# Where the sums of the seven accumulators stand: ahead of the next group's first products, and, in the last group, between the accumulators' own closing products

## The chip, the cores and the metric

The kernel runs on one core of one Trainium2 chip. The metric is device time in microseconds (us), as the median of several runs. "The profiled execution" is one run that a hardware profiler recorded; every duration of a single instruction below comes from it. In its rows PE is the engine of the matrix multiplications (TensorE), PEld its loading of weights, DVE is VectorE, ACT is ScalarE, POOL is GpSimd and SP is SyncE, which issues most DMAs here.

## The reference: what is computed

A state space scan over 4 batches, 8 heads, 768 positions and 32 values per head gives a matrix of 3072 tokens by 256 features. A feed-forward block follows it, all in float32:

```
h = x @ w_in                            # 3072x256 @ 256x2048
g = h * (1.0 / (1.0 + np.exp(-1.702 * h)))
out = (g @ w_out).astype(np.float32)    # 3072x2048 @ 2048x256
```

The scan itself works on chunks. With `L` the decay between two positions of a chunk and `state` what is carried on from earlier chunks, its core is

```
CB = np.einsum('bhin,bhjn->bhij', Cc, Bc)
y_intra = np.einsum('bhij,bhjd->bhid', CB * L, xc)
y_inter = np.einsum('bhin,bhnd->bhid', Cc, state) * decay_to_i[:, :, :, None]
state = decay_full[:, :, None, None] * state + np.sum(Bx, axis=2)
```

## The kernel before

The 3072 tokens are cut into six groups of 512 (`g` = 0 to 5). A group of tokens comes out of the scan as two pairs of 128-position chunks (`p`, two per group), whose result is written transposed into `yT`. The scan of a pair is cut into steps: `turn` transposes B and C on PE (tiles `tp`, then `BT`, `CT`, `CsT`), `gain` multiplies B by x on PE (tile `A`, line L438), `keep` turns `A` into the carried state `S` on DVE (L452, L459), `score` multiplies C by B on PE (tile `cb`, L412), `weigh` multiplies `L` by `cb` on DVE (L422), and `finish` makes `y` on PE and copies it to `yT` on ACT.

The feed-forward block of a group has 16 blocks of 128 hidden features. `hidden` (L508) multiplies `yT` by one block of `w_in` into a PSUM tile `h`, and ACT applies the gelu into `gT` (L511); a step H0 to H7 makes two of them. In the groups 1 to 5 the second matrix product is made in Winograd's form of Strassen's scheme: for each pair of blocks `j` (steps P0 to P7) DVE first makes sums of `gT` (`mix_g`, tile `mg`, L557 to L559), sums of `w_out` are made once (`mix_w`, tile `mw`), and `product` (L575) makes seven matrix products of 128 by 128 by 256 instead of eight, one for each of seven accumulators. The program has one matmul for each of them, the profile two records. The accumulators lie in one PSUM tile `acc` of four banks, two to a bank, the seventh alone, and add up over the eight `j`. When the last `j` is done, `combine` puts the seven together: one ACT copy of accumulators 0 and 3 into the tile `u` (L586), then five DVE sums (L592) that read the other accumulators and write the result `c`. `give` transposes `c` on PE (tiles `oT`, L600), scales it on ACT into `ob` (L603) and stores it.

The four banks of `acc` are the only buffer of that size (`area`, one buffer with the tag "cb"): `cb` of the scan's next pair and `acc` take turns in it. So `score` of the next pair can't begin before `combine` has read all of `acc`. The other four banks (`bank`, tag "ff") go round among `h`, `tp`, `A`, `y` and `oT`.

Every engine runs its instructions in the order in which the program was written (`in_order` adds that as a constraint); nothing reorders them. The order around the change is a list of steps for each group, `H0, H1, H2, P0, H3, P1, ... H7, P5, P6, P7`, and a table `after[g]` of further work behind each step. In the groups 2 to 5 the work behind H0 is first `combine` of the group before, then, where there is a next group, `score` and `weigh` of its first pair; behind H1 stand `mix_g(g, 0)`, `give` of the group before, `score` and `weigh` of the second pair. Behind P5 and P6 stand `turn`, `gain` and `keep` of a pair two groups on. After the last group `combine` and `give` follow without anything else.

Of the kernel before, what the change touches and what calls it, by code (L numbers as in the profile page):

```python
# [8 lines left out]
FP32 = mybir.dt.float32  # L9
U32 = mybir.dt.uint32  # L10
AF = mybir.ActivationFunctionType
ALU = mybir.AluOpType
# [3 lines left out]
P = 128  # L16
# [18 lines left out]
def kernel(  # L35
# [28 lines left out]
    nc = tc.nc  # L64
# [4 lines left out]
    NB, NH, S, D = x.shape  # L69
# [3 lines left out]
    T = NB * S  # L73
# [285 lines left out]
    def turn(p):  # L359
        turn_only(p)  # L360
        since_start(p)
# [6 lines left out]
    def area(name):  # L368
        return ps.tile([P, R, 4 * P], FP32, tag="cb", name=name, bufs=1)
# [48 lines left out]
    def weigh(p):  # L418

        L, cb = Ls[p], st[p].pop("cb")  # L420
        Lv = L.rearrange("p k r q i -> p k r (q i)")
        nc.vector.tensor_tensor(out=Lv, in0=Lv, in1=cb.rearrange("p r k e -> p k r e"),  # L422
                                op=ALU.mult)
# [134 lines left out]
        nc.vector.tensor_tensor(out=t[:, 2], in0=B[:, 1, 1], in1=t[:, 0], op=ALU.subtract)  # L558
        nc.vector.tensor_tensor(out=t[:, 3], in0=B[:, 1, 0], in1=t[:, 2], op=ALU.subtract)  # L559

    def product(g, j):
        if j == 0:
            acc[g] = area(f"acc{g}").rearrange("p r (t e) -> p r t e", t=2)
        B = gT.pop((g, j)).rearrange("p i (t e) -> p i t e", t=2)
        T = mixed_g.pop((g, j))
        A, S = w_out[:, 2 * j:2 * j + 2], mixed_w[j]
        for r, t, lhsT, rhs in (
                (0, 0, A[:, 0, :P], B[:, 0, 0]),
                (0, 1, A[:, 1, :P], B[:, 1, 0]),
                (1, 0, S[:, 1], T[:, 2]),  # L570
                (1, 1, S[:, 0], T[:, 0]),
                (2, 0, S[:, 2], T[:, 1]),
                (2, 1, S[:, 3], B[:, 1, 1]),
                (3, 0, A[:, 1, P:], T[:, 3])):
            nc.tensor.matmul(out=acc[g][:, r, t], lhsT=lhsT, rhs=rhs,  # L575
                             start=(j == 0 and t == 0), stop=(j == NF // 2 - 1),
                             skip_group_check=True)

    def combine(g):


        a = acc.pop(g).rearrange("p r t e -> p (r t) e")
        u = ffn.tile([P, 4, HT], FP32, tag="gT", name=f"u{g}", bufs=NF // 2)
        c = done[g] = ffn.tile([P, 2, 2, HT], FP32, tag="gT", name=f"c{g}", bufs=NF // 2)

        nc.scalar.activation(u[:, 0:4:3], a[:, 0:4:3], AF.Copy)  # L586
        for o, v, w in ((u[:, 2], a[:, 2], u[:, 0]),
                        (u[:, 1:3], a[:, 3:5], u[:, 2:3].to_broadcast([P, 2, HT])),
                        (c[:, 0], a[:, 1:6:4], u[:, 0:2]),
                        (c[:, 1, 1], u[:, 2], u[:, 3]),  # L590
                        (c[:, 1, 0], a[:, 6], u[:, 2])):
            nc.vector.tensor_tensor(out=o, in0=v, in1=w, op=ALU.add)  # L592

    def give(g):
        c = done.pop(g)
        for t in range(2):
            o = bank(f"oT{g}_{t}").rearrange("p (k e) -> p k e", k=2)
            for k in range(2):
                for i in range(2):
                    nc.tensor.transpose(out=o[:, k, i * P:(i + 1) * P],  # L600
                                        in_=c[:, i, t, k * P:(k + 1) * P], identity=ident)
            ob = out_tile(g, t)
            nc.scalar.activation(ob, o, AF.Copy, scale=1.0 / GELU_SCALE)  # L603
            store(g, t, ob)
# [45 lines left out]
    def at(places, i, *work):  # L650
        places.setdefault(i, []).extend(work)
# [26 lines left out]
    for g in range(1, NG):  # L678
        n, places = (g + 1) * PG, after[g]
        chunks = range((g + 2) * CG, (g + 3) * CG) if g + 2 < NG else ()  # L680
        if g == 1:
            def late(p):
                gain(p)
                keep(p)
                score(p)
                weigh(p)

            at(places, "H0", lambda: decay(2 * CG), lambda: decay(2 * CG + 1), lambda: turn(n1))
            n1 = n
# [34 lines left out]
    for g in range(1, NG):  # L724
        if g + 2 < NG:
            for k in range(PG):
                load((g + 2) * PG + k)
            for b in range(NB):
                if (g + 2) * CG <= b * NC < (g + 3) * CG:
                    spread_rows(b)  # L730
                    at(after[g], "P4", lambda b=b: clip_rows(b), lambda b=b: decay_rows(b))
        ahead = 5 if g == 1 else 3
        steps = [f"H{j}" for j in range(ahead)]
        for j in range(NF // 2):
            steps += [f"P{j}"] + ([f"H{j + ahead}"] if j + ahead < NF // 2 else [])
# [12 lines left out]
    combine(NG - 1)  # L748
    give(NG - 1)

    in_order(tc)
# [30 lines left out]
```

## Time and profile before

| what | value |
|---|---|
| median of three runs | 430.02 us (429.22 to 431.66) |
| the profiled execution's own time | 429.2 us |
| its span, from the first to the last instruction | 427.5 us |
| PE busy | 395.3 us, 92% of the span |
| DVE busy | 232.5 us, 54% |
| ACT busy | 119.9 us, 28% |
| mean granted clock of PE | 0.947 |

The time that lies around the span is 429.2 - 427.5 = 1.7 us. Busy times are sums over the whole span; a wait in one place doesn't show in them. The granted clock is the share of full speed that PE was given; at 0.50 a matmul takes twice as long.

### The profile page before, as it was taken

How to read it: one execution, taken by the hardware profiler on the slowest of the kernel's cores; microseconds unless marked ns; L12 is line 12 of the kernel's file. 1: busy time of each engine (PE TensorE's matmuls, PEld its weight loads, DVE VectorE, ACT ScalarE, POOL GpSimd, SP SyncE). 2: the span in 40 equal slices, each digit the busy share in tenths (PEclk: the TensorE clock that was granted, in tenths of full speed). 3: DMA queues.
4: the chain of work that ended last, by engine and by line, in shares of the span. 5: the costliest groups of instructions: out<-in, count | busy, mean ns of one | idle time of the engine just before them, and what ended most of it. 6: DMA issues, size and time to landing. Idle time of an engine off the chain costs nothing.

```text
span 427.5 us, 5052 instructions
## 1 busy us (share of the span) xinstructions
PE 395.3 (92%) x2006; PEld 251.5 (59%) x2006; DVE 232.5 (54%) x372; ACT 119.9 (28%) x227; POOL 8.9 (2%) x28
## 2 busy tenths in 40 slices
PE   6789995989999999699999699999699999999993
PEld 2354454868556687266658256668346667566672
DVE  3899889683879694543573462573262221232212
ACT  4129964340422112132122131212122121231211
POOL 4100000000000000000000000000000000000000
PEclk9559996999999999899999899999889999999997
DMA  8889919500897000078000051000010000010001
GB/s 182 169 179 247 328 52 164 179 0 2 131 263 105 20 0 2 0 245 100 2 1 0 2 174 73 0 0 2 0 49 2 2 0 0 0 51 0 0 2 49
DMA packets 86070, 29.65 MB, mean 69 GB/s; under 512 B 75744, under 2 KB 79008, under 8 KB 86048
## 3 DMA queue, kind: packets, MB, share of 16 engines
q1 hardware_dynamic: 83968, 29.07, 28.5%
q10 hardware_dynamic: 2080, 0.26, 0.4%
q8 instruction: 16, 0.26, 0.3%
q14 instruction: 6, 0.05, 0.0%
HBM read 26.08 MB, written 3.24 MB: 69 GB/s over the span
## 4 chain that ended last, share of the span: by engine, by line
PE 84%; DVE 8%; issue 2%; DMA 2%; ACT 2%; SPq 1%; DVEq 0%; POOL 0%; ACTq 0%; POOLq 0%
PE h L508 39%; PE acc L575 29%; PE o L527 5%; PE cb L412 3%; PE y L488 2%; DVE c L592 2%; PE y L480 1%; DMA af<-in_a_dram 1%; DVE u L592 1%; SPq L110 1%; PE oT L600 1%; DVE L L275 1%; PE tp L379 1%; PE ab L292 1%; ACT u L586 1%
## 5 line engine op out<-in xcount | busy, mean ns | idle before, releaser
L508 PE MATMUL h<-yT,w_in 128*128 128x512 f32 x384 | 177.3, 609 | 0.3 <-ACT yT L494 0.3
L508 PEld LDWEIGHTS h<-yT,w_in 128*128 128x128 f32 x384 | 73.6, 195 | 81.8 <-issue 77.2
L511 ACT ACTIVATE gT<-h 128x512 f32<-128x512 f32 x96 | 57.0, 595 | 204.5 <-PE h L508 162.1
L557 DVE TENSOR_TENSOR mg<-gT 128x512 f32<-128x512 f32 x40 | 27.5, 688 | 91.5 <-ACT gT L511 88.4
L575 PE MATMUL acc<-mg,mw 128*128 128x256 f32 x240 | 58.3, 379 | 0.0
L575 PEld LDWEIGHTS acc<-mg,mw 128*128 128x128 f32 x240 | 45.6, 190 | 6.2
L575 PE MATMUL acc<-gT,w_out 128*128 128x256 f32 x160 | 42.1, 386 | 0.0
L275 DVE TENSOR_TENSOR_SCAN L<-a,idents 128x1024 f32<-128x1024 f32 x18 | 41.1, 2283 | 0.0
L575 PEld LDWEIGHTS acc<-gT,w_out 128*128 128x128 f32 x160 | 29.6, 190 | 15.2 <-issue 11.5
L527 PE MATMUL o<-w_out,gT 128*128 128x256 f32 x128 | 32.3, 410 | 0.0
L422 DVE TENSOR_TENSOR L<-L,cb 128x2048 f32<-128x2048 f32 x10 | 22.9, 2285 | 16.1 <-PE cb L412 16.1
L527 PEld LDWEIGHTS o<-w_out,gT 128*128 128x128 f32 x128 | 25.6, 206 | 5.0 <-issue 1.2
L412 PE MATMUL cb<-CT,BT 32*128 32x256 f32 x160 | 17.0, 495 | 11.5 <-DVE c L592 11.5
L592 DVE TENSOR_TENSOR u<-acc,u 128x256 f32<-128x256 f32 (+1 forms) x10 | 5.6, 558 | 36.3 <-ACT u L586 36.1
L575 PE MATMUL acc<-gT,mw 128*128 128x256 f32 x80 | 23.8, 379 | 0.0
L575 PE MATMUL acc<-mg,w_out 128*128 128x256 f32 x80 | 23.8, 379 | 0.0
L412 PEld LDWEIGHTS cb<-CT,BT 32*128 32x128 f32 x160 | 10.9, 231 | 16.3 <-issue 14.7
L559 DVE TENSOR_TENSOR mg<-gT,mg 128x256 f32<-128x256 f32 x40 | 17.0, 425 | 1.4
L558 DVE TENSOR_TENSOR mg<-gT,mg 128x256 f32<-128x256 f32 x40 | 17.0, 424 | 1.4
L575 PEld LDWEIGHTS acc<-gT,mw 128*128 128x128 f32 x80 | 15.2, 190 | 2.1
L575 PEld LDWEIGHTS acc<-mg,w_out 128*128 128x128 f32 x80 | 15.2, 190 | 2.1
L151 ACT ACTIVATE z<-e,edge 128x512 f32<-128x512 uint32 x16 | 11.4, 713 | 12.8 <-DVE e L147 12.8
(87 smaller groups left out, 278.7 us busy)
## 6 DMA issues: line engine op xcount, KB each, us to landing
a<-scratch SPq DMA_DIRECT2D x18, 512.0 KB, 5.5
bits<-in_moe_w_in_dram SPq DMA_DIRECT2D x8, 512.0 KB, 6.0
bits<-in_moe_w_out_dram SPq DMA_DIRECT2D x8, 512.0 KB, 3.8
out_dram<-ob SPq DMA_DIRECT2D x12, 256.0 KB, 2.1
x<-in_x_dram SPq DMA_DIRECT2D x22, 128.0 KB, 3.0
b<-in_B_dram SPq DMA_DIRECT2D x24, 64.0 KB, 5.5
c<-in_C_dram SPq DMA_DIRECT2D x24, 64.0 KB, 3.1
af<-in_a_dram SPq DMA_DIRECT2D x4, 384.0 KB
```

Source lines behind the costliest of these rows:

```text
L151: nc.scalar.activation(z, e, AF.Relu, scale=-8.0, bias=edge[:, 0:1])
L275: nc.vector.tensor_tensor_scan(out=Ls[p][:, k].rearrange("p r q i -> p (r q i)"), data0=ra[n], data1=idents.rearrange("p h i -> p (h i)"), ...
L412: nc.tensor.matmul(out=cb[:, r, k], lhsT=BT[rows, k], rhs=CT[rows, k].rearrange("p q i -> p (q i)"), start=True, stop=True, tile_position= ...
L422: nc.vector.tensor_tensor(out=Lv, in0=Lv, in1=cb.rearrange("p r k e -> p k r e"), op=ALU.mult)
L508: nc.tensor.matmul(out=h, lhsT=w_in[:, k, f * P:(f + 1) * P], rhs=yT[g][:, k], start=(k == 0), stop=(k == NK - 1))
L511: nc.scalar.activation(gT[g, j][:, i], h, AF.Silu, scale=GELU_SCALE)
L527: nc.tensor.matmul(out=o[k // 2][:, k % 2], lhsT=gT[g, f // 2][:, f % 2, k * P:(k + 1) * P], rhs=w_out[:, f], start=(f == 0 and k % 2 == 0 ...
L557: nc.vector.tensor_tensor(out=t[:, 0:2], in0=B[:, :, 1], in1=B[:, 0], op=ALU.subtract)
L558: nc.vector.tensor_tensor(out=t[:, 2], in0=B[:, 1, 1], in1=t[:, 0], op=ALU.subtract)
L559: nc.vector.tensor_tensor(out=t[:, 3], in0=B[:, 1, 0], in1=t[:, 2], op=ALU.subtract)
L575: nc.tensor.matmul(out=acc[g][:, r, t], lhsT=lhsT, rhs=rhs, start=(j == 0 and t == 0), stop=(j == NF // 2 - 1), skip_group_check=True)
L592: nc.vector.tensor_tensor(out=o, in0=v, in1=w, op=ALU.add)
```

## The change

`combine` is called right behind the step list of its group, and no longer behind H0 of the next group. So on ACT its copy stands ahead of the gelu of the next group's first two `h`, and on DVE its five sums stand ahead of what the next group does there. `gain` and `keep` of the second pair, which stood behind P6, move behind H0 of the next group, ahead of `score` of the first pair. The order of two of the five sums is swapped (`c[:, 1, 1]` now precedes `c[:, 0]`), and `give` now takes the second half of the features first.

In the last group the products of P5, P6 and P7 are taken out of the step list. They are made behind it, accumulator by accumulator in the order 0, 3, 2, 4, 1, 5, 6, each for `j` = 5, 6, 7, with those steps of `combine` in between whose accumulators are complete. `give` follows.

```
-    def product(g, j):
+    def product(g, j, only=range(7)):
...
+        for i in only:
+            lhsT, rhs = terms[i]
+            nc.tensor.matmul(out=acc[g][:, i], lhsT=lhsT, rhs=rhs,
+                             start=(j == 0 and i % 2 == 0), stop=(j == NF // 2 - 1),
...
+        sums = ((u[:, 2], a[:, 2], u[:, 0]),
+                (u[:, 1:3], a[:, 3:5], u[:, 2:3].to_broadcast([P, 2, HT])),
+                (c[:, 1, 1], u[:, 2], u[:, 3]),
+                (c[:, 0], a[:, 1:6:4], u[:, 0:2]),
+                (c[:, 1, 0], a[:, 6], u[:, 2]))
+        for i in steps:
+            if i:
+                o, v, w = sums[i - 1]
+                nc.vector.tensor_tensor(out=o, in0=v, in1=w, op=ALU.add)
...
-        for t in range(2):
+        for t in (1, 0):
...
-            at(places, "H0", lambda g=g: combine(g - 1))
             at(places, "H1", lambda g=g: mix_g(g, 0), lambda g=g: give(g - 1))
             if g + 1 < NG:
-                at(places, "H0", lambda n=n: score(n), lambda n=n: weigh(n))
+                at(places, "H0", lambda n=n: gain(n + 1), lambda n=n: keep(n + 1),
+                   lambda n=n: score(n), lambda n=n: weigh(n))
...
-                at(places, f"P{5 + k}", lambda p=p: turn(p), lambda p=p: gain(p),
-                   lambda p=p: keep(p))
+                at(places, f"P{5 + k}", lambda p=p: turn(p))
+                if k == 0:
+                    at(places, "P5", lambda p=p: gain(p), lambda p=p: keep(p))
...
-            else:
+            elif g < NG - 1 or j < 5:
                 product(g, j)
...
-    combine(NG - 1)
+        if g < NG - 1:
+            combine(g)
+
+    for i, n in ((0, ()), (3, (0,)), (2, (1,)), (4, (2, 3)), (1, ()), (5, (4,)), (6, (5,))):
+        for j in range(5, NF // 2):
+            product(NG - 1, j, (i,))
+        if n:
+            combine(NG - 1, n)
     give(NG - 1)
```

The order on ACT where group 1 ends and group 2 begins (`u1` is the copy of group 1's accumulators, `gT2_0` and `gT2_1` are the gelu of group 2's first four `h`). Before:

```order
L511 ACTIVATE gT2_0_1289<-h2_0_1290 128x512
L511 ACTIVATE gT2_0_1289<-h2_1_1294 128x512
L586 ACTIVATE u1_1298<-acc1_1072 128x2x256
L511 ACTIVATE gT2_1_1316<-h2_2_1317 128x512
L511 ACTIVATE gT2_1_1316<-h2_3_1321 128x512
```

Now:

```order
L586 ACTIVATE u1_1255<-acc1_1072 128x2x256
L511 ACTIVATE gT2_0_1283<-h2_0_1284 128x512
L511 ACTIVATE gT2_0_1283<-h2_1_1288 128x512
L511 ACTIVATE gT2_1_1316<-h2_2_1317 128x512
L511 ACTIVATE gT2_1_1316<-h2_3_1321 128x512
```

The copy moved past two gelus. The five sums on DVE, which wait for it, follow right behind it in both programs.

The order on PE in the same place (`A7` is `gain` of the second pair, `cb6` is `score` of the first). Before:

```order
L379 MATMUL tp7_1236<-ident_149,c7_877 128x128 x2
L438 MATMUL A7_1248<-x7_878,Be7_1162 32x64 x8
L575 MATMUL acc1_1072<-gT1_7_1140,w_out_77 128x256 x2
L575 MATMUL acc1_1072<-mg1_7_1232,mw3_1171 128x256 x3
L575 MATMUL acc1_1072<-gT1_7_1140,mw3_1171 128x256
L575 MATMUL acc1_1072<-mg1_7_1232,w_out_77 128x256
L508 MATMUL h2_0_1290<-yT2_985,w_in_76 128x512 x2
L508 MATMUL h2_1_1294<-yT2_985,w_in_76 128x512 x2
L412 MATMUL cb6_1306<-CT6_1207,BT6_1205 128x256 x8
```

Now:

```order
L379 MATMUL tp7_1236<-ident_149,c7_877 128x128 x2
L573 MATMUL acc1_1072<-gT1_7_1140,w_out_77 128x256 x2
L573 MATMUL acc1_1072<-mg1_7_1232,mw3_1171 128x256 x3
L573 MATMUL acc1_1072<-gT1_7_1140,mw3_1171 128x256
L573 MATMUL acc1_1072<-mg1_7_1232,w_out_77 128x256
L508 MATMUL h2_0_1284<-yT2_985,w_in_76 128x512 x2
L508 MATMUL h2_1_1288<-yT2_985,w_in_76 128x512 x2
L438 MATMUL A7_1292<-x7_878,Be7_1162 32x64 x8
L412 MATMUL cb6_1306<-CT6_1207,BT6_1205 128x256 x8
```

Only `A7` changed its place: from before the last products to between the two `h` and `cb6`. The same holds where groups 2 and 3 end.

The closing products of the last group on PE, with the semaphores that each waits for in brackets. Before, the last of the three `j`:

```order
L575 MATMUL acc5_2254<-gT5_7_2346,w_out_77 128x256 [waits Activation_49] x2
L575 MATMUL acc5_2254<-mg5_7_2362,mw3_1171 128x256 [waits DVE_49]
L575 MATMUL acc5_2254<-mg5_7_2362,mw3_1171 128x256 x2
L575 MATMUL acc5_2254<-gT5_7_2346,mw3_1171 128x256
L575 MATMUL acc5_2254<-mg5_7_2362,w_out_77 128x256 [waits DVE_49]
```

Now, from the last product of accumulator 3 on: three each of accumulators 2, 4 and 1, and, behind those of accumulator 5, the first of accumulator 6:

```order
L573 MATMUL acc5_2254<-mg5_7_2355,mw3_1171 128x256 [waits DVE_49]
L573 MATMUL acc5_2254<-mg5_5_2322,mw2_1129 128x256 [waits Activation_49]
L573 MATMUL acc5_2254<-mg5_6_2342,mw3_1171 128x256
L573 MATMUL acc5_2254<-mg5_7_2355,mw3_1171 128x256 [waits DVE_49]
L573 MATMUL acc5_2254<-mg5_5_2322,mw2_1129 128x256 [waits DVE_49]
L573 MATMUL acc5_2254<-mg5_6_2342,mw3_1171 128x256
L573 MATMUL acc5_2254<-mg5_7_2355,mw3_1171 128x256
L573 MATMUL acc5_2254<-gT5_5_2306,w_out_77 128x256 [waits DVE_49]
L573 MATMUL acc5_2254<-gT5_6_2326,w_out_77 128x256
L573 MATMUL acc5_2254<-gT5_7_2346,w_out_77 128x256
...
L573 MATMUL acc5_2254<-mg5_5_2322,w_out_77 128x256 [waits DVE_49]
```

Each accumulator's last product now comes one after the other, and four of the first products wait for ACT or DVE: those of accumulator 2 (for ACT), 4, 1 and 6 (for DVE). Their operands of `j` = 5 had been waited for by earlier rows or come from another engine, so these waits belong to the copy and the sums that read `acc`.

More of the change, by code (lines that the diff above doesn't have):

```diff
@@ L559, in mix_g @@
         nc.vector.tensor_tensor(out=t[:, 3], in0=B[:, 1, 0], in1=t[:, 2], op=ALU.subtract)
-    def product(g, j):
+    def product(g, j, only=range(7)):
         if j == 0:
-            acc[g] = area(f"acc{g}").rearrange("p r (t e) -> p r t e", t=2)
-        B = gT.pop((g, j)).rearrange("p i (t e) -> p i t e", t=2)
-        T = mixed_g.pop((g, j))
+            acc[g] = area(f"acc{g}").rearrange("p r (t e) -> p (r t) e", t=2)
+        B = gT[g, j].rearrange("p i (t e) -> p i t e", t=2)
+        T = mixed_g[g, j]
@@ L566, in product @@
         A, S = w_out[:, 2 * j:2 * j + 2], mixed_w[j]
[L567 to L576, printed above, removed]
-                             skip_group_check=True)
@@ L579, in combine @@
[L579 to L592, printed above, removed]
+        terms = ((A[:, 0, :P], B[:, 0, 0]), (A[:, 1, :P], B[:, 1, 0]), (S[:, 1], T[:, 2]),
+                 (S[:, 0], T[:, 0]), (S[:, 2], T[:, 1]), (S[:, 3], B[:, 1, 1]),
+                 (A[:, 1, P:], T[:, 3]))
@@ new lines, in product, with combine @@
+        for i in only:
+            lhsT, rhs = terms[i]
+            nc.tensor.matmul(out=acc[g][:, i], lhsT=lhsT, rhs=rhs,
+                             start=(j == 0 and i % 2 == 0), stop=(j == NF // 2 - 1),
+                             skip_group_check=True)
+    def combine(g, steps=range(6)):
+        a = acc[g]
+        if 0 in steps:
+            u = ffn.tile([P, 4, HT], FP32, tag="gT", name=f"u{g}", bufs=NF // 2)
+            c = ffn.tile([P, 2, 2, HT], FP32, tag="gT", name=f"c{g}", bufs=NF // 2)
+            done[g] = u, c
+            nc.scalar.activation(u[:, 0:4:3], a[:, 0:4:3], AF.Copy)
+        u, c = done[g]
+        sums = ((u[:, 2], a[:, 2], u[:, 0]),
[7 more added lines that the diff above has]
+                nc.vector.tensor_tensor(out=o, in0=v, in1=w, op=ALU.add)
@@ L594, in give @@
     def give(g):
-        c = done.pop(g)
-        for t in range(2):
+        u, c = done.pop(g)
+        for t in (1, 0):
             o = bank(f"oT{g}_{t}").rearrange("p (k e) -> p k e", k=2)
```

## The prediction

> **What bounds the kernel now.** I read the page's first parts, then the chain of waits, then the list of waits, then the timeline where a group ends. The page says that PE is the bound:
>
> ```profile
> span 427.5 us, 5052 instructions
> PE 395.3 (92%) x2006; PEld 251.5 (59%) x2006; DVE 232.5 (54%) x372; ACT 119.9 (28%) x227; POOL 8.9 (2%) x28
> PE 84%; DVE 8%; issue 2%; DMA 2%; ACT 2%; SPq 1%; DVEq 0%; POOL 0%; ACTq 0%; POOLq 0%
> ```
>
> The last row is the chain: 84% of it is PE's own work, so only the remaining places can give without making products cheaper. The chain around the end of group 1 (start, length, what) and the matching row of the list of waits (total, times, longest):
>
> ```profile
> 168.59 3.45 PE h L508 x8
> 172.08 0.47 issue
> 172.55 0.60 ACT u L586
> 173.18 0.43 DVE u L592
> 173.64 0.70 DVE u L592
> 174.36 1.37 DVE c L592 x3
> 175.86 1.15 PE cb L412 x16
> 177.01 5.33 PE h L508 x8
> ...
> PE cb L412 <- DVE c L592: 11.5, 3, 3.8
> ```
>
> PE finishes its eight records of `h` at 172.04, then stands until 175.86, because `cb` goes into the banks that the sums still read. The sums are late for a reason on ACT: `acc` was complete at about 168.6, but the copy stands behind the gelu of `h1`, which waits for `h`. This happens three times.
>
> The views by stretch show what follows (length; busy PE, PEld, DVE, ACT, POOL; granted clock). The first three rows are the waits, then come in turn `cb` and `h` behind the wait, and the same work for the second pair without a wait:
>
> ```profile
> 172.04:175.86 3.82, 0.00 (x0) 0.03 (x1) 2.47 (x5) 1.08 (x2) 0.00 (x0) 1.00 0.00 0
> 238.07:241.89 3.82, 0.00 (x0) 0.03 (x1) 2.47 (x5) 1.09 (x2) 0.00 (x0) 1.00 0.00 0
> 304.05:307.87 3.82, 0.00 (x0) 0.03 (x1) 2.47 (x5) 1.08 (x2) 0.00 (x0) 0.90 0.00 0
> 175.86:182.17 6.31, 6.31 (x24) 2.91 (x25) 3.74 (x4) 0.60 (x1) 0.00 (x0) 0.73 0.00 0
> 183.14:187.85 4.71, 4.71 (x26) 2.16 (x25) 3.43 (x4) 1.41 (x3) 0.00 (x0) 1.00 0.78 197
> 241.89:248.15 6.26, 6.26 (x24) 3.10 (x25) 3.74 (x4) 0.60 (x1) 0.00 (x0) 0.73 0.01 3
> 249.12:253.83 4.71, 4.71 (x26) 2.16 (x25) 3.43 (x4) 1.40 (x3) 0.00 (x0) 1.00 0.83 195
> 307.87:315.43 7.56, 7.56 (x25) 3.65 (x26) 3.74 (x4) 0.60 (x1) 0.00 (x0) 0.60 0.00 0
> ```
>
> So every wait is paid twice: PE idles 3.82 us, and then the clock falls, and the same work takes 6.31, 6.26 and 7.56 us instead of 4.71.
>
> **Part 1: the sums ahead of the next group, at three boundaries.** When are they done now? The end of the program shows the same copy and sums with nothing ahead of them (start, length):
>
> ```profile
> 418.57 0.59 PE L575 MATMUL acc<-mg,w_out 128*128 128x256 f32 x2
> 419.26 0.60 ACT L586 ACTIVATE u<-acc 128x512 f32<-128x512 f32 x1 [8.53 <-PE acc L575]
> 419.89 1.15 DVE L592 TENSOR_TENSOR u<-acc,u 128x256 f32<-128x256 f32 x2 [7.52 <-ACT u L586]
> 421.07 0.69 DVE L592 TENSOR_TENSOR c<-acc,u 128x512 f32<-128x512 f32 x1
> 422.01 0.42 DVE L592 TENSOR_TENSOR c<-acc,u 128x256 f32<-128x256 f32 x1
> 422.48 1.14 PE L600 MATMUL oT<-ident,c 128*128 128x128 f32 x7 [0.34 <-DVE c L592]
> 423.07 1.19 ACT L603 ACTIVATE ob<-oT 128x512 f32<-128x512 f32 x2 [3.21 <-PE oT L600]
> ```
>
> The copy starts 0.10 us after the last product ends (418.57 + 0.59 = 419.16) and the sums end at 422.43, 3.27 us after it. At the first boundary the last product ends at 168.6, so the sums end at 171.9. PE is busy with `h` until 172.04 and then with `A`, which the change puts there. What that costs stood in the trace at P6:
>
> ```profile
> 164.94 0.43 PE L438 MATMUL A<-x,Be 128*32 128x64 f32 x16
> ```
>
> About 0.4 us, taken from P6 and spent here, so it adds nothing. `cb` can start at about 172.4, with the sums 0.5 us ahead of it. The wait is gone: 3 x 3.82 = **11.46 us**. If the sums were up to 0.5 us later, `A` would still cover them; the cover without `A` is only 0.14 us, about the 0.13 us from the last sum to `cb` before (174.36 + 1.37 to 175.86). From below I take 11.0, from above 11.46.
>
> What is late next? On DVE `keep` now stands between the sums and `weigh`, and waits for `A`; behind it queue `weigh`, then `mix_g`. `keep` took 1.13 us at P6 (its first and its last row), `weigh` takes 2.29:
>
> ```profile
> 166.59 0.48 DVE L452 TENSOR_TENSOR S<-A,own 128x128 f32<-128x128 f32 x2
> 167.37 0.35 DVE L459 SCALAR_TENSOR_TENSOR S<-S,since 128x128 f32<-128x128 f32 x1
> 184.35 2.29 DVE L422 TENSOR_TENSOR L<-L,cb 128x2048 f32<-128x2048 f32 x1 [3.48 <-PE cb L412]
> ```
>
> `A` ends at 172.4, `keep` at 173.9, `cb` at 173.5, so `weigh` starts 0.4 us late and ends at 176.2. Who needs it first is the second `cb`, which PE reaches after `cb` (1.1), `h` (3.6) and `oT` (1.0), at 178.1. The next product needs `mg`, for which the page has 0.69 + 2 x 0.42, so it is done by 177.7; PE came to that product at 189.35, and will at 189.35 - 3.82 - 1.60 = 183.9. Both covers are over 1.5 us; nothing is added. The SP queue only follows: its stores and loads keep their order and hang on `oT`'s copies, which move with PE.
>
> **The clock** is the second term. If PE no longer idles, `cb` and `h` run at 4.71: 1.60 + 1.55 + 2.85 = **6.00 us**. Evidence that a short pause doesn't cost clock, and that unbroken work doesn't either:
>
> ```profile
> 89.85 0.43 PE L438 MATMUL area<-x,Be 128*32 128x64 f32 x16 [1.76 <-DVE CsT L396]
> 88.10:89.90 1.80, 0.05 (x4) 0.05 (x8) 1.66 (x4) 1.46 (x5) 0.00 (x0) 1.00 0.00 0
> 320.00:366.00 46.00, 46.00 (x235) 31.74 (x234) 10.59 (x21) 7.97 (x16) 0.00 (x0) 1.00 0.00 1
> ```
>
> A pause of 1.76 us kept 1.00; the three of 3.82 did not. Bounds: 0 if the dips have another cause, 6.00 as measured; I take 6.00, since each dip begins during or just behind its wait. The Trainium skill says on its page "TensorE: Matmul & The Clock Gate", section "What's actually happening", that an idle window of about 3.4 us halves the clock until about one busy window has passed; this trace agrees, with 3.82 us of idling ahead of each dip. By that figure a dip would cost about half of 3.4 us, 5.1 us for three as an estimate, and the sum below would be 0.9 us smaller.
>
> **Part 2: the boundary between groups 4 and 5** has no scan and no `cb`. There `h` of both H0 and H1 covers the sums almost entirely:
>
> ```profile
> 372.92 0.27 PE L600 MATMUL oT<-ident,c 128*128 128x128 f32 x1
> 373.40 0.98 PE L600 MATMUL oT<-ident,c 128*128 128x128 f32 x7 [0.21 <-DVE c L592]
> 374.22 3.60 PE L508 MATMUL h<-yT,w_in 128*128 128x512 f32 x8
> ```
>
> From `oT` to the next `h` it is 1.30 us here; elsewhere `oT` fills 0.97 (between the stretches above, 182.17 to 183.14, and again 248.15 to 249.12), where nothing waits. Gain **0.33 us** (0 to 0.45).
>
> **Part 3: the end.** One would expect a gain: with the sums between products, only the last sum would follow the last product. In the frame of the old trace, PE could issue the next instruction at 419.0 (two records of 3.02 / 14 = 0.216 us after 418.57; that row stands below), and then come four `oT` (0.5), the other four behind the last sum (0.26 + 0.42 + 0.1 after 419.0, then 0.4), and two copies of 0.6: the last copy ends about 1.9 us after the products, at 420.9 instead of 424.26. That would be 3.4 us.
>
> But four of the products now wait: accumulator 2 for the ACT copy, 4, 1 and 6 for the sum that was issued just before. Each turns PE and ACT or DVE into a chain. A wait lasts from PE's free slot to the reader's start (419.26 - 419.0 = 0.26), plus the reader, plus its way back (422.43 to 422.48 there, 0.13 at `cb`; I take 0.10): copy 0.60 + 0.36 = 0.96; first sum 0.43 + 0.36 = 0.79; second 0.70 + 0.36 = 1.06; the wide one 0.69 + 0.36 = 1.05. Together 3.86. And products behind a pause take 3.22 us per seven, against 3.02 in a row:
>
> ```profile
> 189.35 3.22 PE acc L575 x14
> 197.85 3.02 PE acc L575 x14
> ```
>
> I put 0.1 us on each restart (bounds 0 and 0.2), so 4.26 (3.5 to 4.8). The new end is 419.0 + 4.26 + 1.9 = 425.16 against 424.26: a **loss of 0.9 us** (0.1 to 1.5). Only the one sum that reads no accumulator and part of `oT` are hidden; all else that was serial stays serial, with four extra trips between the engines. Cover and cost change hands again if the waits aren't there: then the 3.4 us gain stands.
>
> **Sum.** 11.46 + 6.00 + 0.33 - 0.9 = 16.9 us. The profiled execution took 429.2, so it would take 412.3. The median of the runs is 430.02, 0.8 above it; applied to that, **413.1 us**.
>
> **The rivals.**
>
> *The tail overlaps after all* (4%). For it: no product needs a sum's result. Against: the rows of the changed order name the waits. Time 413.1 - 4.3 = 408.8.
>
> *The clock falls in the closing products* (12%). There PE would be busy about 1.3 us in every 2.3. The trace has no such stretch late in the program; the pause of 1.76 us kept the clock, which speaks against it, but it stood alone. If the clock halves after the second wait, nine products of 0.43 and the `oT` double: + 4.4, 417.5. The Trainium skill, same page, section "A second HAM failure mode: psum-queue depth-cycling", says that many tiny idle gaps between groups of matmuls can make the clock swing; this is the rule that speaks against the change.
>
> *The wait at `cb` shrinks but stays* (5%): the copy starts only behind the first gelu.
>
> ```profile
> 170.39 0.60 ACT L511 ACTIVATE gT<-h 128x512 f32<-128x512 f32 x1 [4.17 <-issue]
> ```
>
> Then it would start at 171.0, the sums would end near 174.1, and PE would wait 1.7 us three times, too short for a dip by the pause above: 413.1 + 5.1 = 418.2. The order on ACT speaks against it.
>
> *The dips stay without the waits* (5%): 413.1 + 6.0 = 419.1. For it: `A` and `cb` use 32 rows or columns and may count as little work. Against: 183.14 to 187.85, the same `cb` behind `oT`, had 1.00.
>
> *Slower: the clock granted to PE sinks under unbroken load* (3%). From 172 to 424 PE would have no pause of a microsecond left; each per cent of clock is 2.5 us there, so from 7% on it eats the gain. At 0.90 it is 413.1 + 25 = 438. Against: 46 us without a pause at 1.00, above.
>
> **How the numbers follow.** My forecast has 71%, with 410.5 to 415.5 of its own. The range reaches to the falling clock of the closing products above and halfway to the overlapping tail below: 409.5 to 417.5. A measurement tells 0.5%, about 2.1 us, from no change. Forecast and the first four rivals are all faster by more; of the last, 1 in 3 ends within 0.5%. I leave 1% more for an unforeseen stall that eats just this gain: faster 0.96, same 0.02, slower 0.02.
>
> **What would show it.** Right: no row of `cb` waiting for `c`, clock 1.00 in every stretch behind a boundary, the copy some 0.1 us after the last product of groups 1 to 4, and in the last group four rows of `acc` waiting 0.8 to 1.1 us for `u` or `c`, with `ob` ending no nearer to the end of the `h` products than before. Wrong: a new wait at `weigh` or `mg`, a clock below 1.00 without a pause, or closing products without gaps.

## The result, and the profile after

The changed kernel takes **412.34 us** (median of 4 runs, 411.26 to 413.2) against 429.62 us (4 runs, 428.01 to 431.66) of the kernel before on the same chip: a ratio of 0.9594, with a 95% interval of 0.9544 to 0.9644. The forecast was 413.1. A second measurement on another chip gave 411.85 us and 0.9567 (0.9537 to 0.9597). The profiled execution took 411.26 us, with a span of 409.5 and a mean granted clock of 0.967, against 429.2, 427.5 and 0.947.

From the page after: the span, the busy time of the engines, and the shares of the chain that ended last. Then, from the list of waits (total, times, longest), all rows in which PE waits for the accumulators or their sums.

```profile
span 409.5 us, 5050 instructions
PE 388.7 (95%) x2006; PEld 248.0 (61%) x2006; DVE 233.2 (57%) x372; ACT 120.3 (29%) x227; POOL 8.9 (2%) x28
PE 87%; DVE 6%; SPq 2%; issue 2%; DMA 2%; ACT 1%; POOL 0%; DVEq 0%; ACTq 0%; POOLq 0%
...
PE acc L573 <- DVE u L596: 1.4, 2, 0.8
PE acc L573 <- DVE c L596: 0.8, 1, 0.8
PE acc L573 <- ACT u L586: 0.7, 1, 0.7
```

PE makes the same 2006 records in 388.7 us instead of 395.3: most of the 6.6 us between them are matmuls that no longer run at a low clock. The row of 11.5 us, in which `cb` waited for `c`, has no successor. Four waits of PE are new, all in the closing products; they come to 0.7 + 1.4 + 0.8 = 2.9 us. Gone with the old end is the row in which `oT` waited for `c` (3.2 us in all, 2.7 of it at the end).

The timeline where group 1 ends shows what took the wait's place (start, length, engine, line, operation, tiles, shape; in brackets the idle time before and what ended it):

```profile
168.68 0.60 ACT L586 ACTIVATE u<-acc 128x512 f32<-128x512 f32 x1 [1.91 <-PE acc L573]
...
170.83 1.01 DVE L596 TENSOR_TENSOR c<-acc,u 128x512 f32<-128x512 f32 x2
171.94 0.43 PE L438 MATMUL A<-x,Be 128*32 128x64 f32 x16
172.30 1.15 PE L412 MATMUL cb<-CT,BT 32*128 32x256 f32 x16
173.52 2.29 DVE L422 TENSOR_TENSOR L<-L,cb 128x2048 f32<-128x2048 f32 x1
177.88 1.15 PE L412 MATMUL cb<-CT,BT 32*128 32x256 f32 x16
```

The sums end at 171.84, while PE is still in `h`; `A` covers another 0.4 us, and `cb` starts at 172.30 without a wait. `weigh` ends at 175.81, 2.1 us before the second `cb`.

The views by stretch, for `cb` and `h` behind the first and the third boundary (length; busy PE, PEld, DVE, ACT, POOL; granted clock; DMA share and rate), and for the closing products:

```profile
172.30:177.08 4.78, 4.78 (x33) 2.46 (x27) 4.54 (x8) 0.94 (x2) 0.00 (x0) 1.00 0.00 0
292.83:297.53 4.70, 4.70 (x26) 2.38 (x27) 4.13 (x6) 0.98 (x2) 0.00 (x0) 1.00 0.00 0
394.04:404.65 10.61, 7.71 (x33) 5.67 (x33) 2.23 (x4) 0.60 (x1) 0.00 (x0) 1.00 0.01 2
```

The clock is 1.00 in all three, and `cb` and `h` take 4.7 to 4.8 us where 6.31 and 7.56 stood. It holds in the last row too, although PE is busy there for only 7.71 of 10.61 us.

To see how much each stage gave, take the start of `h` in each group from the chain of waits, of before (group 2 begins at 168.59, a row of the prediction) and of after:

```profile
234.62 3.45 PE h L508 x8
300.60 3.45 PE h L508 x8
366.22 3.45 PE h L508 x8
410.10 9.08 PE acc L575 x42
```

```profile
168.58 3.43 PE h L508 x8
228.81 3.43 PE h L508 x8
289.14 3.43 PE h L508 x8
348.16 6.87 PE h L508 x16
391.61 2.60 PE acc L573 x12
```

| stage | before | after | difference | by the prediction's terms |
|---|---|---|---|---|
| up to the end of group 1 | 168.59 | 168.58 | -0.01 | 0 |
| first boundary and group 2 | 66.03 | 60.23 | -5.80 | -5.42 (3.82 + 1.60) |
| second boundary and group 3 | 65.98 | 60.33 | -5.65 | -5.37 (3.82 + 1.55) |
| third boundary and group 4 | 65.62 | 59.02 | -6.60 | -6.67 (3.82 + 2.85) |
| last boundary, group 5 up to P4 | 43.88 | 43.45 | -0.43 | -0.33 |
| closing products to the end of the span | 17.40 | 17.89 | +0.49 | +0.9 |
| sum | 427.5 | 409.5 | -18.0 | -16.9 |

The timeline of the end, in the order of the accumulators, from accumulator 2 on:

```profile
394.30 0.60 ACT L586 ACTIVATE u<-acc 128x512 f32<-128x512 f32 x1 [2.05 <-PE acc L573]
394.95 1.56 PE L573 MATMUL acc<-mg,mw 128*128 128x256 f32 x6 [0.75 <-ACT u L586]
397.10 1.56 PE L573 MATMUL acc<-mg,mw 128*128 128x256 f32 x6 [0.59 <-DVE u L596]
399.44 1.56 PE L573 MATMUL acc<-gT,w_out 128*128 128x256 f32 x6 [0.78 <-DVE u L596]
...
403.08 1.56 PE L573 MATMUL acc<-mg,w_out 128*128 128x256 f32 x6 [0.79 <-DVE c L596]
405.12 1.23 ACT L607 ACTIVATE ob<-oT 128x512 f32<-128x512 f32 x2 [10.23 <-PE oT L604]
```

From the first closing product to the end of `ob` it was 424.26 - 410.10 = 14.16 us before, and is 405.12 + 1.23 - 391.61 = 14.74 now. The new end is not shorter but 0.58 us longer.

### The profile page after: what moved, and what is told of

Its sections match the earlier page's. It is cut to its first block, busy times and chain, and to the rows that moved or that the text cites. A ratio compares the mean times of both kernels' runs of the same rounds, so it can differ in the third digit from the quotient of the medians.

```text
span 409.5 us, 5050 instructions
## 1 busy us (share of the span) xinstructions
PE 388.7 (95%) x2006; PEld 248.0 (61%) x2006; DVE 233.2 (57%) x372; ACT 120.3 (29%) x227; POOL 8.9 (2%) x28
## 4 chain that ended last, share of the span: by engine, by line
PE 87%; DVE 6%; SPq 2%; issue 2%; DMA 2%; ACT 1%; POOL 0%; DVEq 0%; ACTq 0%; POOLq 0%
PE h L508 40%; PE acc L573 30%; PE o L527 6%; PE cb L412 3%; PE y L488 2%; DMA af<-in_a_dram 2%; PE y L480 1%; SPq L110 1%; PE oT L604 1%; DVE L L275 1%; PE tp L379 1%; PE ab L292 1%; PE A L438 1%; DVE p L169 1%; DVE m L167 1%
## 5 line engine op out<-in xcount | busy, mean ns | idle before, releaser
L508 PE MATMUL h<-yT,w_in 128*128 128x512 f32 x384 | 172.6, 595 | 0.4 <-ACT yT L494 0.4
L508 PEld LDWEIGHTS h<-yT,w_in 128*128 128x128 f32 x384 | 71.7, 190 | 78.3 <-issue 73.7
L573 PEld LDWEIGHTS acc<-gT,w_out 128*128 128x128 f32 x160 | 29.5, 190 | 16.1 <-issue 11.5
L412 PE MATMUL cb<-CT,BT 32*128 32x256 f32 x160 | 15.0, 451 | 0.0
L315 DVE TENSOR_TENSOR_SCAN L<-ab,idents 128x512 f32<-128x512 f32 x12 | 13.7, 1206 | 1.6 <-PE ab L292 1.6
```

Of the source, the lines that this page charges most:

```text
L315: nc.vector.tensor_tensor_scan(out=flat[p][:, r], data0=ab, data1=idents.rearrange("p h i -> p (h i)")[:, :2 * Q * P], initial=0.0, op0=AL ...
L412: nc.tensor.matmul(out=cb[:, r, k], lhsT=BT[rows, k], rhs=CT[rows, k].rearrange("p q i -> p (q i)"), start=True, stop=True, tile_position= ...
L508: nc.tensor.matmul(out=h, lhsT=w_in[:, k, f * P:(f + 1) * P], rhs=yT[g][:, k], start=(k == 0), stop=(k == NK - 1))
L573: nc.tensor.matmul(out=acc[g][:, i], lhsT=lhsT, rhs=rhs, start=(j == 0 and i % 2 == 0), stop=(j == NF // 2 - 1), skip_group_check=True)
```

## The experiments

Theory: the gain is the removed wait at three boundaries and the clock that fell behind it. The new end costs about what its overlap gains, because the closing products wait for the readers of the other accumulators. Rivals: the gain comes from the end, or from the moved `A`; the dips are no result of the waits; the end is decided by the clock rather than by its order.

**The change once more.** The unchanged edit, as the reference for three kernels that ran beside it on the same chip: the boundaries alone, `gain` and `keep` back, and the four tiles. Every ratio below is against the kernel before on the chip of that run (430.38 us on this one).

> The change itself, as the yardstick for the others on the same chip. Expected 412.3 us against 429.6 before, ratio 0.960; in its trace no row of cb waits for c, the clock is 1.00 behind every boundary, and four rows of the closing products wait 0.6 to 0.8 us on PE.

Measured: 411.85 us (411.21 to 412.14), ratio 0.9567 (0.9537 to 0.9597), span 410.3.

**The boundaries alone**, with the old end: the last group's products stay in the step list, and all sums follow.

```
-            elif g < NG - 1 or j < 5:
+            else:
                 product(g, j)
...
-    for i, n in ((0, ()), (3, (0,)), (2, (1,)), (4, (2, 3)), (1, ()), (5, (4,)), (6, (5,))):
...
+    combine(NG - 1)
```

> Only the sums and gain at the boundaries are moved; the last group's products and sums stand as before (all products, then the copy and five sums). If the four waits of the closing products cost what the first trace of the change shows, about 0.5 us more than the order before, this is 0.5 us faster than the change: 411.8 us, and from the first closing product to the end of the last ob it takes 14.3 us or a little less, not 14.9. Rival, the interleaved end is worth its keep (3.4 us): this would be slower than the change, 415.7 us. Rival, the clock at the end decides: in the order before the clock had sunk by the last copies, and if that costs, the two are level.

Measured: 411.36 us (409.57 to 412.82), ratio 0.9559 (0.9526 to 0.9593), span 408.9. So the boundaries hold the whole gain. The medians lie 0.49 us apart, as expected, but the intervals overlap, and the trace does not carry it: from the first closing product to the end of the span it is 408.9 - 391.06 = 17.84 us here, and 410.3 - 392.41 = 17.89 in the change. Why the old end is not better by the 0.5 us that separated it from the new one in the first two profiles shows in its rows, from the chain and from the view by stretch:

```profile
391.06 9.08 PE acc L573 x42
403.12 1.98 PE oT L604 x8
...
403.12:405.09 1.97, 1.96 (x8) 1.56 (x8) 0.27 (x1) 0.60 (x1) 0.00 (x0) 0.50 0.00 0
```

PE stands from 400.14 to 403.12, and `oT` then runs at a clock of 0.50: 1.98 us instead of the 1.08 that the eight records take in the change (below, with the four tiles, too). In the kernel before, the row in the prediction has 1.14 us for seven of the eight, at a clock of 0.80. Four more kernels below keep the old end. From the first closing product to the end of `ob` it takes 14.78 us in three of them, with those seven records at 0.50, and 14.06 in the one with three extra products, with the records at 1.00. It is 14.66 here, and the new end takes 14.74 in each of its five traces. So the two ends are about level, for a reason that the prediction did not have: the old one pays with the clock, how much changes from trace to trace, and the new one pays with waits. The 14.16 us of the first profile was one of the shorter draws.

**The end alone**: `combine`, `gain` and `keep` stand where they were, and only the last group is changed.

```
+            at(places, "H0", lambda g=g: combine(g - 1))
...
-        if g < NG - 1:
-            combine(g)
```

> Only the last group's end is changed (closing products accumulator by accumulator, the sums in between); the order at the boundaries is that of before. By the first traces the new end takes 0.5 us longer than the old one: 430.0 + 0.5 = 430.5 us, not to be told from no change in time, and in its trace 14.9 us from the first closing product to the end of the last ob. Rival, the interleaved end gains on its own: 426.6 us.

Measured: 431.07 us (12 runs) against 430.89 (23 runs), ratio 1.0011 (0.9988 to 1.0033): no difference that can be told. Its list of waits and its chain:

```profile
PE cb L412 <- DVE c L596: 11.5, 3, 3.8
...
412.11 2.60 PE acc L573 x12
426.25 0.60 ACT ob L607
```

The waits at `cb` are back in full, and the closing products to the end of `ob` take 426.85 - 412.11 = 14.74 us, the same as in the change. The end as a source of the gain is out.

**`gain` and `keep` back behind P6**, the rest as in the change. This takes away the 0.4 us with which `A` covers the sums.

```
-                at(places, "H0", lambda n=n: gain(n + 1), lambda n=n: keep(n + 1),
-                   lambda n=n: score(n), lambda n=n: weigh(n))
+                at(places, "H0", lambda n=n: score(n), lambda n=n: weigh(n))
...
+                at(places, f"P{5 + k}", lambda p=p: turn(p), lambda p=p: gain(p),
+                   lambda p=p: keep(p))
```

> The change, but gain and keep of the second pair stay behind P6, where they stood before. The sums end 3.3 us after the last product and h takes 3.4, so if A is only a small cover, PE waits at cb for nothing or up to 0.2 us at each of three boundaries, and the products of P7 start behind A again, 0.2 us slower by the first traces (3.22 against 3.02): 412.3 + 0.6 to 1.2 = 413 us. Rival, A is what hides the end of the sums: waits of 0.5 us or more show at cb, 414 us or more. Rival, the move of gain costs more on DVE than it gives: faster than the change.

Measured: 412.51 us (410.9 to 413.79), ratio 0.9587 (0.9551 to 0.9623), 0.66 above the change; the intervals overlap. Its chain where group 1 ends:

```profile
165.07 0.36 PE A L438 x16
165.43 3.22 PE acc L573 x14
...
172.08 1.13 PE cb L412 x16
```

`cb` follows `h` without a wait, so the cover of `A` is not needed; the 0.14 us without it suffice. What the move brings is something else: the products of P7 take 3.22 us behind `A`, and 3.02 in the change, where they follow `tp` alone (3.02 in the chain of after, from 165.56 to 168.58). That is 0.2 us at each of three places, 0.6 in all.

**The last group's accumulators in four tiles of one bank each**, with the same seven products in the order 0, 3, 2, 4, 1, 5, 6 and the sums cut to fit. Everything else is as in the change.

```
+            acc[g] = [four.tile([P, 2, HT], FP32, tag=f"q{k}", name=f"q{k}") for k in range(4)]
...
+    close(0, 3)
+    nc.scalar.activation(u[:, 0:4:3], a[0], AF.Copy)
+    close(2)
+    add(u[:, 2], a[1][:, 0], u[:, 0])
+    add(u[:, 1], u[:, 3], u[:, 2])
+    close(4)
...
```

> The change, but the last group's seven accumulators lie in four tiles of one bank each (0 and 3, 2 and 6, 1 and 5, 4), so that a product no longer has to wait for sums that read another bank; one sum reads the copy of accumulator 3 and one more instruction is needed. If the four waits are what the end costs, the closing products take 9.1 us without a gap, the last copy ends 1.9 us behind them, and the time is 4.0 us below the change: 408.3 us. Rival, the chain of sums itself sets the end: DVE is late with the sums, oT waits for it, and the gain stays under 1.5 us: 411 us or more.

Measured: **407.78 us** (407.05 to 409.27), ratio 0.948 (0.9448 to 0.9512), 4.07 below the change, where 4.0 was expected. It is faster than both kernels. The last rows of its chain, and the view by stretch of its closing products:

```profile
400.90 1.08 PE oT L617 x8
402.00 0.60 ACT ob L620
...
391.83:400.90 9.07, 9.07 (x45) 7.93 (x44) 3.94 (x8) 1.19 (x2) 0.00 (x0) 1.00 0.01 2
```

The 42 records run in a row in 9.07 us, while ACT and DVE are busy with the copy and the sums of finished accumulators; `oT` starts at once and at full clock. From the first closing product to the end of `ob` it is 10.77 us, 3.97 less than in the change. No product needs a sum's result, in either kernel. The waits of the change come from the tile: all seven accumulators lie in one, and the program's semaphores hold back a write to one accumulator until the readers of the others are done. A shared bank is not the reason for three of the four: accumulators 4, 1 and 6 wait for sums that read other banks than theirs. Only accumulator 2 shares its bank with one that is being read, 3, which the copy takes. The four tiles also put 3 elsewhere, so for that one wait tile and bank are not told apart.

**Does the wait cause the dip?** In the kernel before, four extra products of ones (results unused) are put ahead of `cb` at each boundary. They leave all dependencies as they are and only shorten the time in which PE idles.

```
-                at(places, "H0", lambda n=n: score(n), lambda n=n: weigh(n))
+                at(places, "H0", lambda: keep_busy(4), lambda n=n: score(n), lambda n=n: weigh(n))
```

> The kernel before, with four extra products of ones (3.4 us on PE, result unused) ahead of cb at the three boundaries and at no other place: cb still starts when the sums are done, but PE no longer idles. If the idling is what lowers the clock, PE's wait is 0.4 us, the clock stays at 1.00 behind it, cb comes at most 0.1 us later than before, and only the 6 us of slow clock are won: 430.0 - 6.0 = 424.0 us. Rival, the clock falls there for another reason (cb and A use 32 rows or columns only): the dips stay, 430 us.

Measured: 423.71 us (423.39 to 424.1), ratio 0.985 (0.9819 to 0.9881). The remaining wait, and `cb` and `h` behind it at the first boundary:

```profile
PE cb L412 <- DVE c L592: 1.2, 3, 0.4
...
176.06 1.15 PE cb L412 x16
177.21 3.63 PE h L508 x8
```

`cb` starts no earlier than without them, since the sums end no earlier, and yet 430.89 - 423.71 = 7.2 us are gone. The idle time caused the dips; that they stay without it is out.

**Two extra products instead of four**, which leave a pause of 2.1 us.

> As the run with four extra products, but with two (1.7 us), which leaves PE idle for 2.1 us at the three boundaries. If a pause of some 2 us keeps the clock, as one of 1.76 us did in the kernel before, this too has 1.00 behind it and 424 us. Rival, 2.1 us are enough for a dip at some boundaries: between 424 and 430 us.

Measured: 426.94 us (424.86 to 428.19, 10 runs), ratio 0.9918 (0.9892 to 0.9944). The expectation of no dip, 424, missed. Its waits, and `cb` and `h` at the three boundaries by stretch (granted clock third from the end):

```profile
PE cb L412 <- DVE c L592: 6.4, 3, 2.1
...
176.43:182.85 6.42, 6.42 (x26) 3.12 (x27) 3.74 (x4) 0.60 (x1) 0.00 (x0) 0.73 0.00 0
242.41:247.19 4.78, 4.78 (x26) 2.48 (x27) 3.50 (x4) 0.60 (x1) 0.00 (x0) 1.00 0.01 3
306.75:313.17 6.42, 6.42 (x26) 3.25 (x27) 3.74 (x4) 0.60 (x1) 0.00 (x0) 0.73 0.00 0
```

A pause of 2.1 us lowers the clock at two boundaries of three, by 1.64 us each, with the same instructions around it.

**The copy one gelu later.** The change, with the copy and the sums only behind the first gelu of the next group: the prediction's rival of the shrunken wait, built on purpose.

> The change, but ACT's copy stands behind the gelu of the next group's first h instead of ahead of it. The copy then starts about 2.3 us later, the sums end at 174.2 in the frame of the first trace, and PE, ready for cb at 172.3, waits about 1.9 us at three boundaries, without a dip of the clock: 412 + 5.7 = 417.7 us. Rival, a pause of 1.9 us lowers the clock as well: 420 us or more. Rival, nothing at PE depends on the place of the copy: 412 us.

Measured: 420.78 us (420.52 to 421.39), ratio 0.9783 (0.9745 to 0.9821), where 417.7 would have meant no dips. Its wait, and `cb` and `h` at the three boundaries by stretch:

```profile
PE cb L412 <- DVE c L596: 5.6, 3, 1.9
...
174.34:180.77 6.43, 6.43 (x26) 3.13 (x27) 4.61 (x8) 0.60 (x1) 0.00 (x0) 0.73 0.00 0
238.10:242.88 4.78, 4.78 (x26) 2.49 (x27) 4.11 (x7) 0.60 (x1) 0.00 (x0) 1.00 0.01 3
300.33:306.80 6.47, 6.47 (x26) 3.07 (x27) 4.14 (x6) 0.60 (x1) 0.00 (x0) 0.74 0.00 0
```

The pauses of 1.9 us dip at two of three boundaries again. So one gelu ahead of the copy costs 420.78 - 411.85 = 8.9 us (against the change, which ran on another chip): 5.6 as waits, and 6.43 + 6.47 - 2 x 4.78 = 3.3 through the clock.

**Three extra products, and two with full products behind the pause.** Two questions stayed open: from which length on a pause costs clock, and whether the pause alone decides or also the thin `cb` (32 rows of the array) that follows it. The first kernel has `keep_busy(3)`. The second has two extra products before the pause and four behind it, ahead of `cb`, that read the finished sums (results unused):

```
+    def after_sums(g, n):
+        t = bank("dense")
+        for i in range(n):
+            nc.tensor.matmul(out=t, lhsT=ident, rhs=done[g][:, 1].rearrange("p t e -> p (t e)"),
+                             start=True, stop=True, skip_group_check=True)
...
+                at(places, "H0", lambda: keep_busy(2), lambda g=g: after_sums(g - 1, 4),
+                   lambda n=n: score(n), lambda n=n: weigh(n))
```

> The kernel before, with three extra products of ones (128x128 by 512 columns, results unused) ahead of cb at each of the three boundaries, between the runs with two and with four. Each extra product takes 0.85 us, so a wait of about 1.3 us should stay at cb where two products left 2.1 and four left 0.4. The clock goes by the length of the pause: does 1.3 us lower it? Theory A (pauses from some 1.8 us on lower the clock, shorter ones do not): clock 1.00 behind all three boundaries, cb and h at 1.15 + 3.63, time 430.0 - 6.2 = 424. Theory B (any pause over 1 us ahead of the small products of cb lowers it, at boundaries where the clock's own beat falls badly): one or two dips of 1.6 us each, 425.5 to 427.

> The run with two extra products (pause 2.1 us), and behind the pause, ahead of cb, four more products of 128x128 by 512 columns that read the finished sums c (results unused), at each of the three boundaries. cb fills 32 of the 128 rows of the array and takes 1.15 us, so it may count as little work and lengthen the pause. Theory A (the pause alone decides): dips stay at about two of three boundaries, and the four products show them (over 2 us instead of 1.8). Theory B (pause plus the thin cb behind it decide): no dips, the four products take 1.8 us, cb 1.15 and h 3.63 at all three boundaries. The time is not the point, as the four products add 3 x 1.8 = 5.4 us: without dips 424 + 5.4 = 429.4, with two dips of 1.6 us about 432.5.

Measured with three: 424.61 us (422.62 to 425.12), ratio 0.9831 (0.9766 to 0.9897). The wait is 1.3 us (3.8 in all), and there is no dip; at the first boundary:

```profile
PE cb L412 <- DVE c L592: 3.8, 3, 1.3
...
177.24:182.01 4.77, 4.77 (x26) 2.48 (x27) 3.50 (x4) 0.60 (x1) 0.00 (x0) 1.00 0.00 0
```

Measured with the full products: 435.16 us (434.46 to 437.37, 10 runs), ratio 1.0107 (1.0078 to 1.0136). The timeline and the stretch of `cb` and `h` at the first boundary (the other two read the same):

```profile
176.91 3.67 PE L313 MATMUL dense<-c,ident 128*128 128x512 f32 x8 [2.12 <-DVE c L599]
...
180.57:185.29 4.72, 4.72 (x27) 2.40 (x27) 3.50 (x4) 0.60 (x1) 0.00 (x0) 1.00 0.00 0
```

The four products took 3.67 us, twice what the expectation put (it counted half of the records of each product), so the time without dips is 424 + 3 x 3.67 = 435.0, and that was measured. After the same pause of 2.1 us there is no dip at any of the three boundaries, neither in the full products nor in what follows. This does not show that what follows the pause counts, because these pauses lie otherwise than those with two extra products. In every trace the clock changes only at edges that are a whole number of 3.413 us apart (worked out in the last section). With two extra products alone, the pauses of the first and the third boundary lie whole between two edges, and the clock is 0.50 from the next edge on; the pause that escaped is cut by an edge into 1.90 and 0.22 us. With the full products an edge cuts each of the three pauses: into 0.65 and 1.48, 0.98 and 1.14, 1.31 and 0.81 us. From edge to edge (length, then busy PE; granted clock third from the end), the stretch that holds the first pause with two products:

```profile
173.92:177.34 3.42, 1.29 (x17) 0.77 (x16) 2.29 (x5) 0.00 (x0) 0.00 (x0) 1.00 0.00 0
```

and the two that share the first pause with the full products:

```profile
172.02:175.43 3.41, 2.77 (x7) 0.95 (x5) 1.14 (x3) 1.10 (x3) 0.00 (x0) 1.00 0.00 0
175.43:178.85 3.42, 1.94 (x5) 1.01 (x6) 1.33 (x3) 0.00 (x0) 0.00 (x0) 1.00 0.00 0
```

PE idles 2.13 us in the first stretch, and 0.65 and 1.48 us in the other two. No stretch with 1.48 us or less was followed by a lower clock in any of the twelve traces, so the place of the pauses explains this run without theory B. The median of the ten runs, near the time without dips, suggests that few of the others dipped either, but no trace shows where their pauses lay. Whether what follows a pause counts stays open.

## Why the prediction was right, point by point

**The wait at `cb`, 11.46 us: right.** The sums were forecast to end at 171.9 and ended at 171.84; `cb` was forecast for 172.4 and came at 172.30, the second `cb` for 178.1 and came at 177.88. `keep` was done at 173.57 instead of 173.9, so `weigh` ended at 175.81 instead of 176.2, and nothing waited for either. The kernel with `gain` back shows that even the smaller cover of 0.14 us held.

**The clock, 6.00 us: right,** and now shown: four extra products that change nothing but PE's idle time bring it back, and with it 7.2 us. The terms themselves vary: the kernel with the end alone had `h` behind the waits at 5.26, 4.24 and 5.42 us with `cb` at 2.09 each time, which makes 2.09 x 3 + 14.92 - 3 x 4.78 = 6.85 us, so 6.0 is one draw of a sum that changes from run to run. That the estimate came so near is in part luck.

**`A` moved at no cost: the sign was right, the size was missed.** The prediction let it cancel. It removes 0.36 us and puts 0.36 us back, but the seven products that stood behind it now take 3.02 us instead of 3.22: 0.6 us in all. A row of 3.22 stood in the prediction, at 189.35, used only for the end. This is most of why the first two stages gave 5.80 and 5.65 instead of 5.42 and 5.37. A further 0.1 us each is in `oT`, which fills 0.87 us (177.08 to 177.95 in the chain of after), where 0.97 stood behind the dips.

**The boundary between groups 4 and 5, 0.33 us: right;** 0.43 was measured.

**The end, a loss of 0.9 us (0.1 to 1.5): the mechanism was right, one term was mis-sized.** PE's free slot for accumulator 2 is 12 x 0.216 us after 391.45, where its records of accumulators 0 and 3 begin, at 394.04, and its start at 394.95: 0.91 (forecast 0.96). The next three, counted in the same way (1.29 us for six records, 2.59 for twelve), are 0.86, 1.05 and 1.05 (forecast 0.79, 1.06, 1.05): 3.87 against 3.86. The restarts, put at 0.1 us each, cost 0.09 together: the closing products grew from 9.08 to 13.04 us, by 3.96. The price of a restart had been read from a row that shows none: the products at 189.35 follow `y` without a pause. That leaves 0.58 instead of 0.9. The 0.58 holds against the old end of the first profile only; against the six traces of the old end, 14.06 to 14.78 us, the new one is anything from 0.7 us longer to level. The four tiles turn the argument round: without the waits the end takes 10.77 us against 14.16 before, 3.39 less. That is the gain of 3.4 us that the prediction gave for the case that "the waits aren't there".

**What would show it** came out as written, but for one number: the bracketed waits are 0.6 to 0.8 us, not 0.8 to 1.1. The profile counts them from the end of the last record and the prediction counted from the free slot; the places and their releasers were right.

**The rivals.** *The tail overlaps* and *the clock falls in the closing products* are both out by the trace: four waits, clock 1.00. The rule that the prediction cited for the second, from the section "A second HAM failure mode: psum-queue depth-cycling" of the page "TensorE: Matmul & The Clock Gate" of the Trainium skill, did not show: four gaps of 0.6 to 0.8 us within 13 us left the clock at 1.00. *The dips stay* is out by the four extra products. *The clock sinks under unbroken load* is out: over the 334 us from 76 to 410 us of the trace of after, the granted clock is 1.00.

*The wait shrinks but stays* did not happen in the change, but the kernel that makes it happen shows a wrong step in it. The prediction priced it at 418.2 us, with pauses of 1.7 us "too short for a dip". The one pause that this rested on, 1.76 us ahead of 89.85, kept the clock in the trace of before, but the same pause at the same place did not in five other traces: in the change once more it ends at 89.51, and from 90.90 to 94.31 the clock is 0.50. Ahead of `cb`, 1.8 to 1.9 us dipped at two of three boundaries, and the time was 420.8. One harmless pause was too little to make a bound. This price had no part in the forecast.

**The sum** was 16.9 us, and the profiled executions differ by 18.0 in their span and the medians by 17.3. Between forecast and spans lie 1.1 us. `A` gives 0.6 of it, `oT` 0.3, the end 0.4 and the last boundary 0.1. About 0.55 goes off again, since the stretch up to the end of group 1 ran level although `A` had left it; that stretch varies by itself (168.03 us with the boundaries alone and 169.38 in the change once more, with the same instructions up to there). The remaining 0.25 us is not assigned.

## What to carry to other kernels

When an engine stands late behind a buffer, look for what the late reader queues behind on its own engine: here one ACT copy stood two gelus too low, and moving it freed 11 us of idle time and 6 us of clock. Splitting a closing computation by accumulators overlaps little while all of them lie in one tile whose readers hold back every writer; with one tile for each bank, the same order gained 4 us. A pause of PE of some 2 us or more deserves a price above its length, since the clock may fall behind it.

## What the hardware did that was not expected

Pauses of PE around 2 us are a grey zone. Ahead of `cb`, pauses of 0.4 and 1.3 us lowered the clock at none of three boundaries each, 1.8 to 1.9 and 2.1 us at two of three each, and 3.8 us at all three. A dip behind the 2 us pauses cost about 1.6 us.

Where a pause lies counts beside its length. In each trace the granted clock changes only at edges a whole number of 3.413 us apart: in the kernel before at 177.42, 180.83, 242.27, 245.68, 307.12 and 313.95, which is 0, 1, 19, 20, 38 and 40 such steps behind the first. So a dip lasts one step or two, and the third boundary lost 2.85 us because its dip took two. The boundaries that escaped are those whose pause an edge cut in two: with two extra products into 1.90 and 0.22 us, with the copy one gelu later into 0.49 and 1.32. Counted over all steps of the twelve traces that begin at full clock, from 80 us on: with less than 1.75 us of idle PE in a step the clock never fell at its end, with 2.1 us or more it always fell, and in between, from 1.75 to 1.98 us, it fell at 8 of 13. What decides among those 13 stays open.

The Trainium skill, page "TensorE: Matmul & The Clock Gate", section "What's actually happening", speaks of an idle window of about 3.4 us. The steps of the traces have that length, but a pause that fills only 1.75 to 2.1 us of one could lower the clock already, and the measurement decides. Thin work such as `cb` (32 rows of the array) behind the pause is not needed for it: with the boundaries alone the clock fell at 402.74, 2.6 us after PE had stopped and before it went on, and at the third boundary of the kernel before 3.09 us into the wait (the 3.82 us of idling that the prediction counts ahead of each dip hold for the first two). Whether thin work adds to a pause, no run here settles.

At the end of the program, PE idled 3.0 us in the kernel with the boundaries alone and made `oT` at 0.50; a tail that keeps PE busy until `oT` (1.08 us in the four tiles) saves that too.
